# Attention values: one 64-partition load per block into a ring, the older half copied on the chip; routing's small products moved to another PSUM tile

## The chip, the cores and the metric

One core of one Trainium2 chip runs the whole program. The metric is device time in microseconds (us) of that core. "Before" stands for the kernel without the change.

## The reference

Two stages in a row, all in float32:

```python
# q, k, v: (4, 8, 768, 64)   batch, heads, tokens, head width
scores = q @ k.T / 8
keep   = (key < 4) | (0 <= query - key < 128)        # 4 sink keys and a window of 128
a      = softmax(where(keep, scores, -1e9))
x      = (a @ v), heads side by side                  # (3072, 512)
# two-level routing, top 1 at both levels, then one expert per token
g      = argmax(x @ w_group)      # 4 groups
e      = argmax(x @ w_expert[g])  # 4 experts in it
out    = p(g) * p(e) * (relu(x @ w1[g, e]) @ w2[g, e])   # 512 -> 1024 -> 512
```

## The kernel before, in words

**Attention (first third of the time).** The 3072 tokens are 24 blocks of 128 queries (`NI`; six per batch entry). One pass of the loop at line 1191, a *turn* below, works on five blocks at once in a software pipeline. In turn `i` the kernel computes the scores of block `i`, the transposes and value products of blocks `a = i-1` and `b = i-2`, the transposes of the output of block `c = i-3`, and the routing logits of block `d = i-4`. Each engine executes its instructions in program order; the order is written by hand (class `Pinned`).

In a turn TensorE (PE) runs `scores` (tile `ps`), `trans(a)` (64x64 transposes of the probabilities into the PSUM tile `tp`), `values(b, 0)` and `values(b, 1)` (into `po`), `logits(d)`, at some turns a routing product, `across(c)` and `sink_t(a)` (both into `tp`). ScalarE (ACT) copies the probabilities out of `tp` (`evac`, tile `pa`), does eight exponentials (`exps`, tile `pt`, four for each half `g` of the heads), copies the logits out (`norm_logits`, tile `lt`) between the two groups of four, and copies `tp` out once more at the end of the turn (`settle`, tile `xT`). VectorE (DVE) does masks and maxima (`maxima`, tiles `sm` and `st`), the division by the softmax sum (`norm`, tiles `rc` and `xt`), and from turn 9 on the routing of finished batches of six blocks, a fixed number of steps per turn (`routing`, `UNITS`). GpSimd (POOL) masks `pa` and `pu` (`affine_select`). SyncE (SP) issues nearly all DMAs from one queue, in program order.

`tp` has one buffer of two PSUM banks. The next turn's `trans` therefore waits until `xT` has been read out of it. Writes and reads of one PSUM bank of a tile are ordered among each other by the framework, even where they touch different columns. Before, the logits and routing's products lie in free columns of `tp` (`misc` at line 213, `logits` at 859).

**The values.** A block of 128 queries is two halves of 64. A half needs its own 64 keys, the 64 before and the 64 before those, plus the sinks. `load_v(i)` fetches a tile of 128 partitions by 2 x 520 floats (520 KB). For half 0 of the block, partitions 0 to 63 hold the block's first 64 tokens and partitions 64 to 127 the last 64 of the block before; for half 1 they hold the second and the first 64 of the block itself. So each 64-token piece is fetched twice, and the layout of the input `vN` carries it twice. `values(b, 0)` multiplies all 128 partitions. When it has read the tile, `load_s` overwrites partitions 64 to 95 with the sinks' values (130 KB), and in the next turn `values(b, 1)` reads partitions 0 to 95 of that tile. Three tiles rotate (`vts`, `vv`).

**End of attention and after it.** Lines 1252 to 1315 finish the last blocks while the first expert's layer 1 begins (`ew`). From turn 17 on, one 512 KB chunk of expert weights per turn is prefetched (`HOOK`, tile `rw`) on the same SP queue. Then the experts' products follow, layer 1 and layer 2 of one expert after another, until the end.

Of the kernel before, what the change touches and what calls it, by code (L numbers as in the profile page):

```python
# [9 lines left out]
F32 = mybir.dt.float32  # L10
# [11 lines left out]
P = 128  # L22
B, H, S, D = 4, 8, 768, 64
NT = S // P
# [6 lines left out]
NE = G * EG  # L31
# [8 lines left out]
SK = slice(D, D + NH)  # L40
# [3 lines left out]
XW = DM + GW  # L44
VW = D + 1
VM = H * VW
NEG = -1.0e30
BIG = 1 << 20
CAPT = [384, 256, 480, 288, 288, 224, 192, 192, 160, 160, 160, 160, 128, 128, 64, 32]
# [16 lines left out]
PRE = 2  # L66
# [25 lines left out]
XS = NDC * D + D  # L92
# [4 lines left out]
MAXB = 6  # L97
# [9 lines left out]
PW = G + NE  # L107
# [43 lines left out]
def moe_attention(tc, kqT, vN, vS, nsw, wg, w1, w2, out):  # L151
    nc = Pinned(tc)
    v = nc.vector
    with ExitStack() as top, ExitStack() as att:
# [37 lines left out]
        nc.gpsimd.memset(act, 0.0)  # L192
        nc.gpsimd.memset(colm[0:1], 1.0)
        nc.gpsimd.memset(kb[:, :, 0:BW], 0.0)
        vts, env, bat = {}, {}, {}

        def bank(pt):
            return pt.tile([P, 4, P], F32, name="tp")
# [11 lines left out]
        def spare():  # L210
            return tail[0].tile([P, 512], F32, name="ph")

        def misc(pt):
            if pt is None:
                return spare() if tail else env["tp"][:, 0, XS:XS + MAXB * NE + NE]
            return bank(pt).rearrange("p a b -> p (a b)")

        rawp = []
# [12 lines left out]
            for h, eng in ((slice(0, HP), nc.sync),) if i else ((slice(0, 2), nc.scalar), (slice(2, HP), nc.sync)):  # L231
                eng.dma_start(kb[:, h, n * BW:(n + 2) * BW], kqT[b, t, :, 0:KB].rearrange("d (h n) -> d h n", h=HP)[:, h])

        def room_v(i):
            vts[i] = wk.tile([P, 2, VM], F32, name="vv", bufs=3)

        def load_v(i):
            room_v(i)
            b, t = divmod(i, NT)
            nc.sync.dma_start(vts[i].rearrange("p f n -> p (f n)"), vN[b, t])  # L240

        def load_s(i):
            nc.sync.dma_start(vts[i - 1][SK].rearrange("p f n -> p (f n)"), vS[i // NT])

        for i in range(DEPTH):
            load_q(i)
# [520 lines left out]
        def maxima(i, g):  # L767
            t = i % NT
            e = env[i]
            if t:  # L770
                v.copy_predicated(psb[g][:, :, CW - D:CW], selu[:, None, :].to_broadcast([P, 4, D]), psb[g][:, :, BW - D:BW])
            e["sm", g] = sm = wk.tile([P, 4, SW], F32, name="sm", bufs=2)
            for k in range(4):
                h = head(g, k)
                v.tensor_tensor_reduce(
                    sm[:, k], psb[g][:, k, CW - SW:CW], msk[:, min(t, 2)], -0.125, 3.0e38,
                    ALU.add, ALU.min, e["st"][:, h:h + 1])

        def exps(i, g, ks=range(4)):
            e = env[i]  # L780
            for k in ks:
                h = head(g, k)
                nc.scalar.activation(e["pt"][:, h].rearrange("p (b k) -> p b k", b=2)[:, ::-1],
                                     e["sm", g][:, k].rearrange("p (b k) -> p b k", b=2), AF.Exp, bias=e["st"][:, h:h + 1],
                                     scale=-1.0)
# [43 lines left out]
                    nc.gpsimd.tensor_copy(pu[s % 2][g][SK].rearrange("p h (f q) -> p h f q", f=2),  # L829
                                          xT[SK, None, :, NDC * D:XS].to_broadcast([NH, 4, 2, D]))  # L830

        def values(i, k, gs=(0, 1)):
            rows = slice(0, P) if k == 0 else slice(0 if i % NT else D, D + NH)
            for g in gs:
                pk = env[i]["pT", g][k]
                for h in range(4):
                    for f in range(2):
                        o = slice(f * D, (f + 1) * D)
                        nc.tensor.matmul(po[o, g, h * VW:(h + 1) * VW], pk[rows, h, o],
                                         vts[i - k][rows, f, (4 * g + h) * VW:(4 * g + h + 1) * VW],  # L840
                                         start=k + h == 0, stop=k + h == 4)

        def norm(i):
# [13 lines left out]
                    nc.tensor.transpose(env["tp"][:, j, c * D:(c + 1) * D], env[i]["xt"][r, c * P:(c + 1) * P], ident[r, r])  # L857

        def logits(i):
            env[i]["lg"] = lg = spare()[:, 0:PW] if tail else env["tp"][:, 1, XS:XS + PW]  # L860
            for c in range(NDC):
                for j in range(2):
                    nc.tensor.matmul(lg[j * D:(j + 1) * D], env[i]["xT"][:, j, c * D:(c + 1) * D], wsb[:, c],
                                     start=c == 0, stop=c == NDC - 1)
# [4 lines left out]
        def norm_logits(i):  # L869
            k = max(j for j in range(len(BATCHES)) if bounds[j] <= i)  # L870
            nb, j = BATCHES[k], i - bounds[k]
            if j == 0:
                bat[k] = rk.tile([P, MAXB, PW], F32, name="lt", bufs=2)
            lt = bat[k]
            nc.scalar.copy(lt[:, j], env[i]["lg"])
            del env[i]
            have.add((id(lt), j))
            if j == nb - 1:
                pick = {SNAP: 0, SNAPB: 1, len(BATCHES) - 1: 2}.get(k)
                rb.append([[(id(lt), x) for x in range(nb)], route(bounds[k], nb, lt, pick), None])  # L880
# [303 lines left out]
                yield us  # L1184

        ew = early_work(PARTS[0][0])
        room_v(-1)
        load_s(0)
        load_v(0)
        rest = None  # L1190
        for i in range(NI):
            a, b, c, d = i - 1, i - 2, i - 3, i - 4
            state["clk"] += 3.0
            scores(i, 0)
            scores(i, 1)
            if i + DEPTH < NI:
                load_q(i + DEPTH)
            if a >= 0:
                env["tp"] = pair()
                trans(a)  # L1200
                evac(a, 0)
                evac(a, 1)
            warm(FILL[i] if i < len(FILL) else 0, po[:, 0, 300:492])
            if b >= 0:
                values(b, 0)
                load_s(b + 1)
            if i + DEPTH < NI:
                load_k(i + DEPTH)
            if i == 0:
                load_v(1)  # L1210
            if b >= 0:
                values(b, 1, (0,))
            if d >= 0:
                logits(d)
            routing(1, ("pe",))
            if b >= 0:
                values(b, 1, (1,))
                load_v(i)
            maxima(i, 0)
            exps(i, 0)  # L1220
            if d >= 0:
                norm_logits(d)
            maxima(i, 1)
            routing(PRE, (None, "rd"))
            if b >= 0:
                norm(b)
            if c >= 0:
                across(c)
            if a >= 0:
                sink_t(a)  # L1230
            exps(i, 1)
            if a >= 0:
                settle(c, a)
            if i < NI - 1:
                sink_pack(i)
            if i == 0:
                late_consts()
            if i == 3:
                tables()
            state["clk"] += 3.0  # L1240
            if rest:
                rest()
                rest = None
            put_gates(3)
            if later and not gates:
                gather(*later.pop(0))
            routing(UNITS.get(i, REND), (None, "rd"))
            rest = half.pop()() if half else wjob() if i < NI - 1 else None
            if i in HOOK:
                prefetch(min(RAW, len(raws) + 1))  # L1250
# [27 lines left out]
        sink_t(a)  # L1278
        settle(c, a)
        routing(1, ("pe",))  # L1280
        next(ew)
        if half:
            half.pop()()()
        elif state["done"] < NDC:
            wjob(True)
        values(a, 0)
        logits(c)
        env["tp"] = pair()
        across(b)
        norm_logits(c)  # L1290
        settle(b, None)
        while state["done"] < NDC:
            wjob(True)

# [287 lines left out]
def layout(q, k, v, n_sink, window, moe_w_group, moe_w_expert, moe_w1, moe_w2):  # L1582
    qT = q.reshape(B, HP, 2, NT, P, D).transpose(0, 3, 2, 5, 1, 4).reshape(B, NT, P, HP * P)
    kc = k.reshape(B, H, NT, 2, D, D)
    ks = np.broadcast_to(k[:, :, None, None, :NSK, :], (B, H, NT, 2, NSK, D))
    kx = np.concatenate([ks, ks, kc], axis=4).reshape(B, HP, 2, NT, 2, BW, D)
    kT = kx.transpose(0, 3, 2, 6, 1, 4, 5).reshape(B, NT, P, KB)
    kqT = np.concatenate([kT, qT], axis=3)
    vb = v.transpose(0, 2, 1, 3).reshape(B, NT, 2, D, DM)
    vp = np.concatenate([np.zeros_like(vb[:, :1, 1]), vb[:, :-1, 1]], axis=1)  # L1590
    vN = np.concatenate([np.concatenate([vb[:, :, 0], vp], axis=2),
                         np.concatenate([vb[:, :, 1], vb[:, :, 0]], axis=2)], axis=3)
    vN = np.concatenate([vN.reshape(B, NT, P, 2, H, D), np.ones((B, NT, P, 2, H, 1), v.dtype)], axis=5).reshape(B, NT, P, 2 * VM)
    vS = np.zeros((B, H, NSK, 2, H, VW), v.dtype)
    for h in range(H):
        vS[:, h, :, :, h, 0:D] = v[:, h, :NSK, None, :]
        vS[:, h, :, :, h, D] = 1
    nsw = np.array([n_sink, window], np.int64).view(np.int32)[None]
    wgx = np.concatenate([moe_w_group, np.ascontiguousarray(moe_w_expert.transpose(1, 0, 2)).reshape(DM, NE)], axis=1)
    wg = wgx.reshape(NDC, P, PW).transpose(1, 0, 2).reshape(P, NDC * PW)  # L1600
    return dict(kqT=kqT, vN=vN, vS=vS.reshape(B, H * NSK, 2 * VM), nsw=nsw, wg=wg,
                w1=moe_w1.reshape(NE, DM, F), w2=moe_w2.reshape(NE, F, DM))
# [17 lines left out]
```

## Time and profile before

| | |
|---|---|
| median of three runs | 492.05 us (490.28 to 492.71) |
| the profiled execution, its own time | 491.24 us |
| its span | 489.5 us |
| first scores / last value product start at | 5.1 us / 154.8 us of the span |
| granted TensorE clock, mean | 0.987 |
| busy PE / DVE / ACT / POOL | 464.7 / 366.9 / 309.0 / 167.9 us |
| DMA moved | 117.27 MB, mean 240 GB/s |

How to read it: the busy share of an engine is an average over stages with different limits, so the stretches are read one by one. In a list by time a number in brackets is idle time of the engine just before that instruction, with what ended it. The two rows' starts of the same instruction in successive turns give the length of a turn.

### The profile page before, as it was taken

The numbers are of one execution on the slowest core, as the hardware profiler recorded it, in microseconds if no ns is written. First come the engines' busy times: TensorE is split into PE (matmuls) and PEld (weight loads), VectorE is DVE, ScalarE is ACT, GpSimd is POOL, SyncE is SP. The second block draws the span as 40 slices with busy tenths as digits, with TensorE's granted clock in tenths as the row PEclk, the third lists the DMA queues.
The fourth block names the chain that finished last, engine by engine and source line by source line (L and its number), as shares of the span: only waits on it lengthen the run. The fifth ranks groups of instructions, "written<-read, shape, count | busy, mean of one in ns | idle before, by whom it ended". The sixth has DMA issues, their size and how long they took to land.

```text
span 489.5 us, 14468 instructions
## 1 busy us (share of the span) xinstructions
PE 464.7 (95%) x5427; PEld 390.9 (80%) x5427; DVE 366.9 (75%) x1181; ACT 309.0 (63%) x669; POOL 167.9 (34%) x264
## 2 busy tenths in 40 slices
PE   8999999989778999999999999999999999999993
PEld 6788888878667978988989789669776977977973
DVE  7776897898587689997823776578687997999740
ACT  4787776777484625587623765377456787788740
POOL 3675665764544112512213022212131063104102
PEclk9999999999799999999999999999999999999997
DMA  8699888998955827872963338686849983999200
GB/s 251 208 310 282 260 272 242 300 285 262 323 175 172 307 102 224 277 240 70 396 266 88 108 131 276 189 348 266 313 168 400 398 317 101 388 361 349 104 21 29
DMA packets 58833, 117.27 MB, mean 240 GB/s; under 512 B 8702, under 2 KB 20990, under 8 KB 58754
## 3 DMA queue, kind: packets, MB, share of 16 engines
q1 hardware_dynamic: 54162, 102.85, 62.3%
q0 software_dynamic: 4320, 13.26, 8.2%
q8 instruction: 45, 0.74, 0.6%
q14 instruction: 34, 0.28, 0.2%
q10 hardware_dynamic: 272, 0.15, 0.1%
HBM read 103.45 MB, written 13.03 MB: 238 GB/s over the span
## 4 chain that ended last, share of the span: by engine, by line
PE 73%; DVE 12%; ACT 6%; DMA 5%; issue 3%; SPq 1%; POOL 0%; POOLq 0%; DVEq 0%; ACTq 0%
PE ph L121 32%; PE po L121 29%; PE tp L121 7%; PE ps L121 4%; ACT pt L121 3%; DMA vv<-in_vS 2%; DVE sm L121 2%; DVE wlo L121 2%; SPq L121 1%; DMA kb<-in_kqT 1%; ACT pa L121 1%; DVE xt L121 1%; DVE un L121 1%; ACT whi L121 1%; DMA out<-ot,hidx 1%
## 5 line engine op out<-in xcount | busy, mean ns | idle before, releaser
L121 DVE TENSOR_TENSOR wlo<-rw,whi 128x1024 fp32r<-128x1024 f32 x112 | 134.3, 1219 | 26.5 <-ACT whi L121 25.5
L121 PE MATMUL po<-whi,un 128*128 128x512 f32 (+5 forms) x384 | 127.9, 396 | 0.0
L121 PE MATMUL ph<-un,whi 128*128 128x256 f32 (+9 forms) x576 | 127.6, 312 | 0.0
L121 ACT CAST whi<-rw 128x1024 fp32r<-128x1024 f32 (+1 forms) x115 | 115.3, 1026 | 8.4 <-PE po L121 4.3
L121 POOL DMA_INDIRECT out<-ot,sidx x32 | 42.1, 1316 | 228.4 <-ACT ot L121 88.8
L121 PE MATMUL ph<-un,wlo 128*128 128x256 f32 (+10 forms) x416 | 99.3, 264 | 0.7 <-DVE wlo L121 0.7
L121 PEld LDWEIGHTS ph<-un,whi 128*128 128x128 f32 x576 | 93.6, 189 | 1.2
L121 PEld LDWEIGHTS po<-whi,un 128*128 128x128 f32 (+4 forms) x384 | 70.4, 185 | 25.2 <-issue 6.7
L121 PEld LDWEIGHTS ph<-un,wlo 128*128 128x128 f32 x416 | 76.7, 189 | 1.6 <-DVE wlo L121 0.9
L121 PE MATMUL po<-wlo,un 128*128 128x512 f32 (+6 forms) x200 | 77.5, 389 | 0.0
L121 ACT ACTIVATE pt<-sm,st 128x136 f32<-128x136 f32 x192 | 61.9, 401 | 8.3 <-DVE st L121 8.2
L121 DVE CUSTOM_DVE_ANT_0 sm<-ps,msk 128x136 f32<-128x136 f32 x192 | 45.9, 295 | 5.2 <-PE ps L121 0.2
L121 POOL DMA_INDIRECT xg<-xd,gidx x30 | 33.5, 1115 | 26.2 <-DMA rw<-in_w 12.9
L121 PEld LDWEIGHTS po<-wlo,un 128*128 128x128 f32 (+5 forms) x200 | 36.0, 180 | 7.7
L121 ACT COPY pa<-tp 128x512 f32<-128x512 f32 x48 | 25.8, 589 | 25.2 <-PE tp L121 25.2
L121 POOL COPY pu<-xT 32x512 f32<-32x512 f32 x46 | 28.0, 636 | 39.2 <-ACT xT L121 33.5
L121 PE MATMUL ps<-kb,qb 64*64 64x208 f32 (+1 forms) x768 | 39.3, 345 | 0.5 <-DMA kb<-in_kqT 0.5
L121 DVE TENSOR_TENSOR hc<-ph,hc 128x160 f32<-128x160 f32 (+6 forms) x64 | 21.1, 335 | 22.2 <-ACT hc L121 22.0
L121 PE MATMUL po<-vv,pu 96*64 96x65 f32 (+1 forms) x768 | 32.2, 227 | 3.9 <-DMA vv<-in_vS 3.7
L121 ACT ACTIVATE ot<-po,cg 128x512 f32<-128x512 f32 (+6 forms) x25 | 17.0, 679 | 26.5 <-PE po L121 26.5
L121 ACT ACTIVATE un<-ph 128x256 fp32r<-128x256 f32 (+1 forms) x40 | 15.3, 383 | 26.9 <-PE ph L121 26.2
L121 PEld LDWEIGHTS ps<-kb,qb 64*64 64x64 f32 x768 | 27.5, 139 | 5.8 <-DVE st L121 0.7
(203 smaller groups left out, 686.6 us busy)
## 6 DMA issues: line engine op xcount, KB each, us to landing
rw<-in_w SPq DMA_DIRECT2D x128, 512.0 KB, 6.2
vv<-in_vN SPq DMA_DIRECT2D x24, 520.0 KB, 5.1
kb<-in_kqT SPq DMA_DIRECT2D x23, 288.0 KB, 4.6
qb<-in_kqT SPq DMA_DIRECT2D x24, 256.0 KB, 4.8
xd<-xt SPq DMA_DIRECT2D x24, 256.0 KB, 4.9
vv<-in_vS SPq DMA_DIRECT2D x24, 130.0 KB, 3.8
out<-ot,sidx POOLq DMA_INDIRECT x32, 4.0
xg<-xd,gidx POOLq DMA_INDIRECT x30, 4.0
```

Source lines behind the costliest of these rows:

```text
L121: r = f(*a, **k)
```

## The change

`load_v(i)` fetches each 64-token piece once: 64 partitions by 2 x 520 floats, 260 KB, into partitions 0 to 63 of two slots of a ring of six (`vv`, the same size as the three tiles before). A new step `older(i)` copies, on the chip, the piece before each half into partitions 64 to 127 of its slot: 64 partitions by 1040 floats in one instruction, or in two of 520 where the ring wraps. VectorE does it for blocks 0 to 8, ScalarE from block 9 on. In a turn it stands behind both `maxima` in program order, on ScalarE between the two groups of exponentials, and it needs the load of block `i-1` to have landed.

The logits and routing's small products move from free columns of `tp` to free columns of `po`. The copy of the logits, `lt`, moves from ScalarE to VectorE, behind `norm`. `values(b, 1)` runs without `logits` in its middle, `load_v(i)` is issued behind it and thus ahead of `logits`, and routing's reads of its products are no longer among the two steps taken ahead of `norm`. At the end, `values(a, 0)` comes later.

```diff
+NV = 6
+OLDER = 9
...
-                return spare() if tail else env["tp"][:, 0, XS:XS + MAXB * NE + NE]
+                return spare() if tail else po[:, 0, 4 * VW:4 * VW + MAXB * NE + NE]
...
-        def room_v(i):
-            vts[i] = wk.tile([P, 2, VM], F32, name="vv", bufs=3)
+        vv = wk.tile([P, NV, VM], F32, name="vv", bufs=1)

         def load_v(i):
-            room_v(i)
             b, t = divmod(i, NT)
-            nc.sync.dma_start(vts[i].rearrange("p f n -> p (f n)"), vN[b, t])
+            s = 2 * i % NV
+            nc.sync.dma_start(vv[0:D, s:s + 2].rearrange("p f n -> p (f n)"), vN[b, t])
...
+        def older(i):
+            copy = v.tensor_copy if i < OLDER else nc.scalar.copy
+            s = 2 * i % NV
+            if i % NT == 0:
+                copy(vv[D:P, s:s + 2], vv[0:D, s:s + 2][:, ::-1])
+            elif s:
+                copy(vv[D:P, s:s + 2], vv[0:D, s - 1:s + 1])
+            else:
+                copy(vv[D:P, 0], vv[0:D, NV - 1])
+                copy(vv[D:P, 1], vv[0:D, 0])
...
-            env[i]["lg"] = lg = spare()[:, 0:PW] if tail else env["tp"][:, 1, XS:XS + PW]
+            env[i]["lg"] = lg = spare()[:, 0:PW] if tail else po[:, 1, 4 * VW:4 * VW + PW]
...
-            nc.scalar.copy(lt[:, j], env[i]["lg"])
+            (nc.scalar.copy if tail else v.tensor_copy)(lt[:, j], env[i]["lg"])
...
             if b >= 0:
-                values(b, 1, (0,))
+                values(b, 1)
+                load_v(i)
             if d >= 0:
                 logits(d)
             routing(1, ("pe",))
-            if b >= 0:
-                values(b, 1, (1,))
-                load_v(i)
             maxima(i, 0)
             exps(i, 0)
+            maxima(i, 1)
+            if a >= 0:
+                older(a)
+            routing(PRE, (None,))
+            if b >= 0:
+                norm(b)
             if d >= 0:
                 norm_logits(d)
-            maxima(i, 1)
-            routing(PRE, (None, "rd"))
-            if b >= 0:
-                norm(b)
...
         routing(1, ("pe",))
+        older(a)
...
-        values(a, 0)
         logits(c)
         env["tp"] = pair()
         across(b)
         norm_logits(c)
         settle(b, None)
+        values(a, 0)
```

## Rows read from the trace of the kernel before

**Rows 1.** Busy time by stretch; window, length, engines, granted clock, DMA share, GB/s.

```profile
54.70:113.00 58.30, 54.26 (x1407) 47.10 (x1403) 51.58 (x264) 43.38 (x124) 36.23 (x63) 1.00 0.88 265
113.00:134.00 21.00, 17.80 (x372) 14.76 (x374) 15.07 (x78) 12.59 (x34) 12.54 (x20) 0.84 1.02 319
...
157.00:198.00 41.00, 39.82 (x274) 34.59 (x271) 32.76 (x115) 18.41 (x32) 7.72 (x6) 1.00 0.63 213
```

**Rows 2.** ScalarE in order of time, one turn; start, length, instruction.

```profile
30.39 1.08 ACT L121 COPY pa<-tp 128x512 f32<-128x512 f32 x2 [1.12 <-PE tp L121]
31.34 1.31 ACT L121 ACTIVATE pt<-sm,st 128x136 f32<-128x136 f32 x4
32.55 0.16 ACT L121 COPY lt<-tp 128x20 f32<-128x20 f32 x1
32.61 1.31 ACT L121 ACTIVATE pt<-sm,st 128x136 f32<-128x136 f32 x4
33.82 0.68 ACT L121 COPY xT<-tp 128x640 f32<-128x640 f32 x1
```

**Rows 3.** TensorE in order of time, the same turn.

```profile
29.63 0.71 PE L121 MATMUL tp<-ident,pt 64*128 64x64 f32 x16
...
31.79 0.63 PE L121 MATMUL tp<-wsb,xT 128*64 128x20 f32 x16
...
34.55 0.65 PE L121 MATMUL tp<-ident,pt 64*128 64x64 f32 x14
```

**Rows 4.** Turns from `trans` to `trans`, columns as in rows 1.

```profile
56.31:62.78 6.47, 5.66 (x149) 4.85 (x146) 6.08 (x31) 4.53 (x13) 4.41 (x9) 1.00 0.88 282
62.78:67.94 5.16, 4.80 (x144) 4.27 (x140) 4.84 (x29) 4.32 (x12) 3.28 (x6) 1.00 0.85 244
...
85.35:90.60 5.25, 5.25 (x144) 4.60 (x140) 4.27 (x24) 4.11 (x12) 3.87 (x8) 1.00 0.98 304
...
96.96:101.88 4.92, 4.74 (x143) 4.27 (x139) 4.57 (x27) 4.11 (x12) 3.38 (x7) 1.00 0.78 238
101.88:108.51 6.63, 5.42 (x138) 4.60 (x138) 6.42 (x32) 4.50 (x13) 4.14 (x8) 1.00 1.01 312
...
115.32:120.86 5.54, 5.54 (x142) 4.72 (x138) 4.57 (x23) 4.74 (x13) 3.87 (x8) 1.00 0.97 276
```

**Rows 5.** ScalarE in order of time, the turn from 101.88.

```profile
105.08 1.31 ACT L121 ACTIVATE pt<-sm,st 128x136 f32<-128x136 f32 x4 [1.38 <-DVE st L121]
```

**Rows 6.** TensorE in order of time, the longest turn, from 120.86.

```profile
125.56 1.10 PE L121 MATMUL po<-vv,pu 96*64 96x65 f32 x16 [2.90 <-DMA vv<-in_vS]
...
129.04 3.05 PE L121 MATMUL ps<-kb,qb 64*64 64x208 f32 x32
```

**Rows 7.** Groups by form: engine, operation, tiles, shapes, count, busy us, mean ns, idle before.

```profile
L121 ACT CAST whi<-rw 128x1024 fp32r<-128x1024 f32 x109 | 111.6, 1048 | 8.4 <-PE po L121 4.3 <-DMA rw<-in_w 3.9
...
L121 ACT CAST whi<-rw 128x512 fp32r<-128x512 f32 x6 | 3.7, 620 | 0.0
...
L121 DVE COPY cnt<-tp 128x16 f32<-128x16 f32 x2 | 0.3, 164 | 0.0
...
L121 DVE COPY msk<-msk 128x136 f32<-128x136 f32 x1 | 0.2, 230 | 0.0
```

**Rows 8.** VectorE in order of time, the turn of rows 2.

```profile
31.75 0.29 DVE L121 CUSTOM_DVE_ANT_0 sm<-ps,msk 128x136 f32<-128x136 f32 x1
...
32.96 0.17 DVE L121 TENSOR_SCALAR rc<-po 128x8 f32<-128x8 f32 x1 [0.90 <-PE po L121]
```

**Rows 9.** VectorE in order of time: one operation beside GpSimd's masks, and without them.

```profile
103.43 0.55 DVE L121 TENSOR_TENSOR rm<-req,rs 128x24 f32<-128x24 f32 x1
...
176.70 0.18 DVE L121 TENSOR_TENSOR rm<-req,rs 128x24 f32<-128x24 f32 x1
```

**Rows 10.** Instructions on tile `tp`: who its writers waited for, us and times.

```profile
  ACT lt L121: 8.4, 9
```

**Rows 11.** DMA issues: count, KB each, median us from issue to landing.

```profile
vv<-in_vN SPq DMA_DIRECT2D x24, 520.0 KB, 5.1
...
vv<-in_vS SPq DMA_DIRECT2D x24, 130.0 KB, 3.8
```

More of the change, by code (lines that the diff above doesn't have):

```diff
@@ L194, in moe_attention @@
         nc.gpsimd.memset(kb[:, :, 0:BW], 0.0)
-        vts, env, bat = {}, {}, {}
+        env, bat = {}, {}
         def bank(pt):
@@ L232, in load_k @@
                 eng.dma_start(kb[:, h, n * BW:(n + 2) * BW], kqT[b, t, :, 0:KB].rearrange("d (h n) -> d h n", h=HP)[:, h])
-        def room_v(i):
-            vts[i] = wk.tile([P, 2, VM], F32, name="vv", bufs=3)
+        vv = wk.tile([P, NV, VM], F32, name="vv", bufs=1)
         def load_v(i):
-            room_v(i)
             b, t = divmod(i, NT)
-            nc.sync.dma_start(vts[i].rearrange("p f n -> p (f n)"), vN[b, t])
+            s = 2 * i % NV
+            nc.sync.dma_start(vv[0:D, s:s + 2].rearrange("p f n -> p (f n)"), vN[b, t])
         def load_s(i):
-            nc.sync.dma_start(vts[i - 1][SK].rearrange("p f n -> p (f n)"), vS[i // NT])
+            s = 2 * (i - 1) % NV
+            nc.sync.dma_start(vv[SK, s:s + 2].rearrange("p f n -> p (f n)"), vS[i // NT])
+        def older(i):
[8 more added lines that the diff above has]
+                copy(vv[D:P, 1], vv[0:D, 0])
         for i in range(DEPTH):
@@ L830, in settle, with values @@
                                           xT[SK, None, :, NDC * D:XS].to_broadcast([NH, 4, 2, D]))
-        def values(i, k, gs=(0, 1)):
+        def values(i, k):
             rows = slice(0, P) if k == 0 else slice(0 if i % NT else D, D + NH)
-            for g in gs:
+            for g in range(2):
                 pk = env[i]["pT", g][k]
@@ L839, in values @@
                         nc.tensor.matmul(po[o, g, h * VW:(h + 1) * VW], pk[rows, h, o],
-                                         vts[i - k][rows, f, (4 * g + h) * VW:(4 * g + h + 1) * VW],
+                                         vv[rows, 2 * (i - k) % NV + f, (4 * g + h) * VW:(4 * g + h + 1) * VW],
                                          start=k + h == 0, stop=k + h == 4)
@@ L1186, in moe_attention @@
         ew = early_work(PARTS[0][0])
-        room_v(-1)
         load_s(0)
@@ L1589, in layout @@
     vb = v.transpose(0, 2, 1, 3).reshape(B, NT, 2, D, DM)
[L1590 to L1593, printed above, removed]
+    vN = vb.transpose(0, 1, 3, 2, 4)
+    vN = np.concatenate([vN.reshape(B, NT, D, 2, H, D), np.ones((B, NT, D, 2, H, 1), v.dtype)], axis=5).reshape(B, NT, D, 2 * VM)
     vS = np.zeros((B, H, NSK, 2, H, VW), v.dtype)
```

## The prediction

> **What bounds the kernel now.** I read the busy time by stretch first, then single turns in order of time, then prices. By stretch [rows 1]: behind attention (157 to 198 us) TensorE is busy 39.82 of 41.00 us, so the end of attention hands its delay on one to one. [...] In a plain turn TensorE and ScalarE run neck and neck. ScalarE's chain is closed: it starts 0.76 us after `trans` (30.39 against 29.63), runs `pa`, four exponentials, `lt`, four exponentials and `xT` without a gap until 34.50, and the next `trans` starts 0.05 us later, at 34.55 [rows 2, 3]. That is a turn of 4.92 us, and the reader is to see that nothing on ScalarE in it is slack but the 1.12 us ahead of `pa`. TensorE's own work makes most other turns some 5.2 to 5.5 us. From turn 10 on VectorE has routing to do: turns with much of it take 6.5 to 6.6 us, in which VectorE is busy 6.1 to 6.4 us and ScalarE waits 1.38 us for `st` [rows 4, 5]. [...]
>
> **The copy on ScalarE, turns 10 to 23.** `older` copies 1040 floats per partition. ScalarE's nearest rows are copies of 512 (620 ns) and 1024 (1048 ns) from on-chip memory [rows 7]: 0.836 ns per float, so 1.06 us. Instructions behind each other overlap by 0.1 us (`pa` runs to 31.47, the exponentials start at 31.34; the next start 32.55 lies ahead of 32.65) [rows 2], so the copy adds 0.95 us to the chain; `lt` leaves and gives 0.06 us back (32.55 to 32.61). ScalarE's closed chain becomes 4.92 - 0.06 + 0.95 = 5.81 us. Eleven turns go from `trans` at 56.31 to `trans` at 120.86, 5.87 us on average [rows 4]. Five are shorter than 5.81: 5.16, 5.54 (twice, one shown), 5.25 and 4.92 [rows 4]. Lifted to 5.81 they cost 0.65 + 0.27 + 0.56 + 0.89 + 0.27 = 2.6 us. In the VectorE-bound turns the copy is behind a late `st`, between the two groups of exponentials, and the second group waits for its own maxima; there part of it is free, and part comes on top. On the other hand VectorE can work ahead while ScalarE is late: in a 5.81 us turn it gets 0.3 to 0.9 us that it did not have in the short ones, and the 6.63 us turns shrink. Least: the long turns average out with the short, eleven times 5.81 = 63.9 against 64.55 us, -0.6. Most: 0.95 in each of eleven turns, +10.5. I take +2.0, near the lifted short turns, since the turns that VectorE bounds leave little to average.
>
> **The copy on VectorE, turns 1 to 9.** Its copies take 164 ns for 16 floats and 230 ns for 136 [rows 7], that is 0.55 ns per float and 0.73 us for 1040. VectorE has a hole for it in a plain turn: `sm` ends at 32.04 and `rc` waits 0.90 us for the value products until 32.96 [rows 8]. The copy fits, if the load has landed. If it runs beside GpSimd's masks, which fill that part of the turn, it may wait: the same small operation took 0.55 us there and 0.18 us without them [rows 9], so 0.37 us more, 1.10 us, and 0.20 over in each of seven turns that are not a batch's first. `lt` adds 0.16 us behind `norm` (the row of 16 floats, [rows 7]), where VectorE has the rest of the hole. Bounds 0 and +1.4 us (with 1.04 ns per float, twice the slope, +5); I take +0.5.
>
> [...]
>
> **The load.** `older` is the first reader of `load_v(a)`; before it was `values(a, 0)` in the turn after. The load is issued earlier, right behind `values(b, 1)` and ahead of the 0.63 us of `logits` [rows 3]. The SP queue order is `load_q`, `load_s`, `load_k`, `load_v`, output, so nothing else moves in it. Issue is some 3 us behind `trans`; 5.1 us of landing [rows 11] puts it 8 us behind, and ScalarE reaches `older` 2.9 us into the next turn, 8.7 us behind in a turn of 5.81. VectorE reaches it 2.4 us in, 7.6 us behind. The wait is thus 0 to 0.5 us; behind it stand four exponentials and `xT` on ScalarE, `norm` on VectorE. With half the bytes I take 0.
>
> **DMA.** The saving is 260 KB per turn. At the 319 GB/s of the full stretch [rows 1] that is 0.82 us each; three value loads fall into the 21 us, so up to -2.4 us where DMA sets the time, and nothing elsewhere, because before 113 us the loads land in time. But the load now writes 64 partitions. The sinks' load writes 32, and its 130 KB land in 3.8 us against 5.1 us for 520 KB [rows 11]: a quarter of the bytes, three quarters of the time. Bounds -2.4 and 0; I take -1.2.
>
> **The move out of `tp`.** `across` no longer waits for the reading of `lt` or of routing's products (8.4 us in 9 waits, shared between weight loads and products, so about half as much time) [rows 10]. It would start `sink_t` and the next scores sooner by up to 0.7 us in some five turns. But `xT` now ends later than before on ScalarE, and `trans` waits for `xT`, so the gain is eaten: 0, at best -1.5 us. In `po` the next `values(b, 0)` has to wait for `lt` and for routing's reads on VectorE; these end about 1 us ahead of it. At the end of attention `older(a)` puts 1 us in front of ScalarE's casts, and `values(a, 0)` moves behind; the sinks' load is still the last to land there. 0, at most +1.
>
> **Sum.** +2.0 + 0.5 + 0 - 1.2 + 0 = +1.3 us. On the profiled execution (491.24 us) that is 492.5, on the median (492.05) 493.4. I predict 492.9 us, and call the change within 0.5% (2.5 us), about what a measurement of this kernel tells from no change.
>
> **Rivals.**
>
> *ScalarE's chain sets every turn (slower).* Place: the stretch from turn 10. It decides if VectorE's routing can't work ahead, since both `maxima` and the copy then come in series: in the turn from 101.88 the exponentials start late [rows 5], then copy, exponentials and `xT` follow, +0.9 us. The price is the 2.6 us of the short turns, 0.6 to 0.9 us in four heavy turns (3.0) and a late landing here and there (1): +6.5, about 498 us. For it: ScalarE's chain has no gap [rows 2]. Against: VectorE is busy 51.58 of 58.30 us from 54.7 to 113 us, 5.2 us per average turn [rows 1]. Chance 0.23.
>
> *The DMA stall goes (faster).* The 2.90 us wait goes if the sinks' load lands 3 us sooner, and with it the slow products behind it: 1.4 us of scores alone [rows 6], some 3 us in all with the products ahead. -6 + 1.3 gives 487.3 us. For it: the full queues. Against: ahead of that load in the queue are weights and queries, not values. Chance 0.29.
>
> *A load into 64 partitions holds the DMA engines as long as one into 128.* Then the 1.2 us of relief go: 494.1 us. For it: rows 11. Against: a small load also has a part of its landing that no bytes cause. Chance 0.10.
>
> [...]
>
> **How the numbers follow.** The forecast has 0.38; its own range is 490 to 496 (0.04 faster, 0.26 same, 0.08 slower). The slow rival gives 0.21 slower and 0.02 same, the fast one 0.27 faster and 0.02 same, the third 0.05 and 0.05. Sums: 0.31 faster, 0.35 same, 0.34 slower. The range reaches to both outer rivals and a little beyond: 486 to 499.
>
> **What would show it.** Right: in the changed trace `vv<-vv` takes near 1.05 us on ScalarE and 0.7 to 1.1 on VectorE; plain turns from 10 on are near 5.8 us with `trans` right behind `xT`; VectorE shows no wait for `in_vN`; DMA share in the full stretch falls; no `tp` wait for `lt`. Wrong: turns 10 to 20 below 5.6 us on average (the chain is not closed), or idle time on ScalarE or VectorE ahead of `vv` for `in_vN` (the landing), or the attention's first ten turns longer by over 2 us (the copy does not fit the hole), or a stall near 120 us that is gone or has doubled.

## The result and the profile after

In 20 runs each the changed kernel takes 494.48 us (median; 490.98 to 498.26) and the kernel before 491.74 us: a ratio of 1.0055 with a 95% interval of 1.0028 to 1.0082, that is 2.7 us more. Every ratio below is the time over that of the kernel before, with such an interval behind it. The profiled execution has a span of 492.4 us against 489.5.

The stretches of [rows 1], now of the changed kernel, same columns:

```profile
54.70:113.00 58.30, 49.83 (x1313) 42.97 (x1311) 48.54 (x256) 48.20 (x115) 34.37 (x61) 1.00 0.75 210
113.00:134.00 21.00, 16.85 (x420) 14.49 (x420) 16.77 (x82) 18.20 (x43) 10.38 (x18) 1.00 0.96 266
157.00:198.00 41.00, 41.00 (x325) 35.75 (x320) 37.21 (x119) 19.14 (x33) 5.67 (x5) 1.00 0.66 224
```

In the first stretch every engine but ScalarE does less in the same 58.30 us: TensorE 49.83 us instead of 54.26, ScalarE 48.20 instead of 43.38. The DMA share falls from 0.88 to 0.75. Turns from `trans` to `trans`, as in [rows 4]:

```profile
56.68:64.89 8.21, 5.81 (x150) 4.66 (x146) 7.61 (x35) 5.46 (x14) 3.75 (x7) 1.00 0.74 220
64.89:70.95 6.06, 4.70 (x138) 4.26 (x138) 5.60 (x31) 5.36 (x13) 3.91 (x7) 1.00 0.67 193
...
77.01:83.07 6.06, 5.98 (x144) 5.23 (x144) 3.84 (x24) 5.20 (x12) 1.37 (x3) 1.00 0.67 178
```

Of eleven turns (`trans` at 56.68 to 126.24) nine lie between 6.05 and 6.15 us, one is 6.67 and the first 8.21. Before, the same eleven ran from 4.92 to 6.80 us. One number that keeps coming back, whatever the other engines have to do, is the mark of a closed chain. ScalarE in order of time, the turn from 77.01, beside [rows 2]:

```profile
77.77 1.07 ACT L123 COPY pa<-tp 128x512 f32<-128x512 f32 x2 [0.80 <-PE tp L123]
78.73 1.31 ACT L123 ACTIVATE pt<-sm,st 128x136 f32<-128x136 f32 x4
80.06 1.06 ACT L123 COPY vv<-vv 64x1040 f32<-64x1040 f32 x1
81.14 1.30 ACT L123 ACTIVATE pt<-sm,st 128x136 f32<-128x136 f32 x4
82.35 0.67 ACT L123 COPY xT<-tp 128x640 f32<-128x640 f32 x1
83.83 1.07 ACT L123 COPY pa<-tp 128x512 f32<-128x512 f32 x2 [0.81 <-PE tp L123]
```

The copy costs 1.06 us as worked out. But the exponentials ahead of it end at 80.04 and it starts at 80.06; it ends at 81.12 and the next start at 81.14. Between exponentials and `xT` the usual overlap of 0.1 us is there (82.35 against 82.44). So the copy adds 80.06 to 81.14 and the lost overlap, 1.20 us instead of 0.95, and the loop is 6.06 us. Of the chain of waits ScalarE now holds 10% (before 6%). TensorE's side says the same: what instructions on tile `tp` waited for (us and times):

```profile
  ACT xT L123: 34.0, 33
```

The same row of the kernel before:

```profile
  ACT xT L121: 9.6, 18
```

The wait for `xT` has more than tripled; `lt` of [rows 10] is gone from the list. The copies on tile `vv` (count, lowest/median/highest ns, first and last start), and what they waited for:

```profile
L123 ACT COPY vv<-vv x18: 618/1057/1060, 61.8 to 155.1; 64x1040 f32<-64x1040 f32 x12, 64x520 f32<-64x520 f32 x6
L123 DVE COPY vv<-vv x10: 419/696/1026, 12.5 to 54.3; 64x1040 f32<-64x1040 f32 x8, 64x520 f32<-64x520 f32 x2
...
  DMA vv<-in_vN: 5.2, 6
```

The loads, as in [rows 11], and TensorE in the stall of [rows 6]:

```profile
vv<-in_vN SPq DMA_DIRECT2D x24, 260.0 KB, 5.1
...
vv<-in_vS SPq DMA_DIRECT2D x24, 130.0 KB, 4.1
```

```profile
128.87 1.15 PE L123 MATMUL po<-vv,pu 96*64 96x65 f32 x32 [0.83 <-DMA vv<-in_vS]
...
137.24 1.25 PE L123 MATMUL po<-vv,pu 96*64 96x65 f32 x32 [1.37 <-POOL pu L123]
...
139.30 3.05 PE L123 MATMUL ps<-kb,qb 64*64 64x208 f32 x32
```

Where the 2.9 us of the span come from, by the starts of `trans` and the end of the last value product: up to the tenth `trans` +0.4 (56.31 to 56.68), the eleven turns +5.0 (64.55 to 69.56), the rest of attention -2.1 (34.1 to 32.1 us). That is 3.3 us at the end of attention (155.0 to 158.3), of which the stage behind it gives 0.4 back. These are differences of one trace each. The place alone and the four kernels with a spare copy (below) are the same program up to the tenth turn, and their tenth `trans` starts between 55.12 and 56.62 us: a difference of half a us, such as the +0.4, says nothing by itself.

### The profile page after: what moved, and what is told of

It is laid out like the page before. It is cut to its first block, busy times and chain, and to the rows that moved or that the text cites. A ratio compares the mean times of both kernels' runs of the same rounds, so it can differ in the third digit from the quotient of the medians.

```text
span 492.4 us, 14530 instructions
## 1 busy us (share of the span) xinstructions
PE 463.6 (94%) x5427; PEld 389.7 (79%) x5427; DVE 375.4 (76%) x1211; ACT 323.4 (66%) x667; POOL 167.9 (34%) x264
## 4 chain that ended last, share of the span: by engine, by line
PE 70%; DVE 11%; ACT 10%; DMA 4%; issue 3%; SPq 1%; POOL 0%; POOLq 0%; DVEq 0%; ACTq 0%
PE ph L123 31%; PE po L123 30%; PE tp L123 6%; ACT pt L123 5%; PE ps L123 2%; DMA vv<-in_vN 2%; DVE wlo L123 2%; DVE sm L123 2%; ACT xT L123 1%; ACT vv L123 1%; ACT pa L123 1%; DVE un L123 1%; DVE xt L123 1%; DMA kb<-in_kqT 1%; ACT whi L123 1%
## 5 line engine op out<-in xcount | busy, mean ns | idle before, releaser
L123 POOL DMA_INDIRECT out<-ot,sidx x32 | 43.5, 1361 | 228.1 <-ACT ot L123 90.1
L123 POOL COPY pu<-xT 32x512 f32<-32x512 f32 x46 | 26.9, 611 | 49.2 <-ACT xT L123 44.0
L123 POOL DMA_INDIRECT xg<-xd,gidx x30 | 32.1, 1070 | 24.8 <-DMA rw<-in_w 12.2
L123 ACT COPY hc<-ph 128x160 f32<-128x160 f32 (+6 forms) x64 | 19.4, 304 | 18.1 <-PE ph L123 17.1
L123 PEld LDWEIGHTS tp<-ident,pt 64*128 64x128 f32 x384 | 13.9, 139 | 21.9 <-ACT xT L123 20.7
```

The source lines that it names most:

```text
L123: r = f(*a, **k)
```

## The experiments

**One half alone.** First the move into `po` with its new order, on the old 128-partition loads, without any copy; then the ring with its copies, with logits and routing's products left in `tp`.

```diff
 # kernel before, place and order alone
-  ... else env["tp"][:, 1, XS:XS + PW]
+  ... else po[:, 1, 4 * VW:4 * VW + PW]      # routing's products likewise, lt on VectorE
 # changed kernel, ring alone
-  ... else po[:, 1, 4 * VW:4 * VW + PW]
+  ... else env["tp"][:, 1, XS:XS + PW]       # routing's products likewise, lt on ScalarE
```

> Half of the change: logits and routing's products in po, lt on VectorE, the new order; values loaded as before, 128 partitions, no copy. Theory (ScalarE's chain): the eleven turns take 58 to 60 us, ratio 0.998 to 1.002; the turn from block 10 still long (near 8 us) if routing's later start makes that one. Rival (VectorE): eleven turns near 63 us and ratio 1.004 to 1.006. If the stall near 120 us stays as before, the new load is what shortened it.

> The other half: the ring, the 64-partition load and the copies; logits and routing's products stay in tp, lt on ScalarE, the old order. Theory (ScalarE's chain): copy and lt both in it, 6.1 us per turn, eleven turns 64 us or more, ratio 1.005 to 1.010. Rival (VectorE): eleven turns near 59 us, ratio 1.000 or below.

Measured: place and order alone 488.57 us, ratio 0.9956 (0.9929 to 0.9982); ring alone 498.19 us, ratio 1.0163 (1.0128 to 1.0198). The first is better and the second worse than either theory had it. The change is a gain of 0.4% and a loss. With the place the ring costs 1.0055 - 0.9956, about 1.0% or 4.9 us; without it 1.6%. ScalarE with the ring alone, by time:

```profile
83.79 1.31 ACT L123 ACTIVATE pt<-sm,st 128x136 f32<-128x136 f32 x4
85.11 0.18 ACT L123 COPY lt<-tp 128x20 f32<-128x20 f32 x1
85.31 1.06 ACT L123 COPY vv<-vv 64x1040 f32<-64x1040 f32 x1
86.39 1.30 ACT L123 ACTIVATE pt<-sm,st 128x136 f32<-128x136 f32 x4
```

`lt` stands in the same closed chain, and the eleven turns are 6.12 to 6.90 us. The theories' "eleven turns" near 63.5 us are the ten from the tenth `trans` to the twentieth: 63.49 us in the changed kernel, 58.83 with the place alone, 64.16 with the ring alone, as the theory of ScalarE's chain had them. Place and order alone beats both kernels.

The expectation for the place alone named a test of the smaller loads: if the stall near 120 us stays as before, the new load is what shortened it. It did not stay. With full loads the wait for the sinks' values is 1.82 us instead of 2.90, and the three turns from the twentieth `trans` to the 23rd take 22.0 us instead of 23.4:

```profile
123.87 1.15 PE L121 MATMUL po<-vv,pu 96*64 96x65 f32 x32 [1.82 <-DMA vv<-in_vS]
```

**The copy elsewhere on ScalarE.** Only the turn's ScalarE copy moves, behind `xT`.

```diff
-            if a >= 0:
+            if 0 <= a < OLDER:
                 older(a)
...
                 settle(c, a)
+            if a >= OLDER:
+                older(a)
```

> Only ScalarE's copy moves: from between the two groups of exponentials to behind xT, where ScalarE waits some 0.75 us for the next transposes anyway. Theory (ScalarE's closed chain of 6.06 us sets the turns): the chain drops to about 5.25 us, the eleven turns after turn 10 from 63.5 to some 59 to 60 us, the time by 3 to 4 us, to 0.997 to 1.000 of before. Rival (VectorE: the moved lt and routing's later start): the turns stay near 63 us, ratio 1.005. Rival (landing of the value loads): the later copy waits less, but the loads also come earlier in a shorter turn; at most 1 us better, ratio 1.003 to 1.005.

Measured: 491.26 us, ratio 1.0013 (0.9986 to 1.0040), 0.4% under the changed kernel, whose interval overlaps this one at its edge; the theory had 0.997 to 1.000. The copy still runs and costs the same time; it no longer stands ahead of `trans`. ScalarE by time:

```profile
85.41 0.68 ACT L123 COPY xT<-tp 128x640 f32<-128x640 f32 x1
86.11 1.06 ACT L123 COPY vv<-vv 64x1040 f32<-64x1040 f32 x1
87.45 1.07 ACT L123 COPY pa<-tp 128x512 f32<-128x512 f32 x2 [0.28 <-PE tp L123]
88.41 2.50 ACT L123 ACTIVATE pt<-sm,st 128x136 f32<-128x136 f32 x8
```

It lies in the time in which ScalarE waits for the next `trans` anyway, and the turns are 5.10 to 6.20 us again, with one of 7.10 and one of 8.29 (TensorE idles for 1.67 us in it, for no reason that the trace shows). The ten turns take 61.6 us, against 63.5 in the changed kernel and 59 to 60 expected. In this profile the stall ahead of 136 us grew to 4.96 us, for `pu` from GpSimd (a turn of 12.93 us), so the attention stage as a whole shows less of the gain than the turns do:

```profile
136.04 2.00 PE L123 MATMUL po<-vv,pu 96*64 96x65 f32 x32 [4.96 <-POOL pu L123]
```

**No copy at all.** The changed kernel without `older`; the upper partitions hold zeros, so only the attention stage is read.

> The changed kernel without the copies (the upper partitions hold zeros, so attention's output, routing and the number of tokens per expert differ; only the attention stage is to be read). Theory: turns of 5.2 to 5.6 us where VectorE has little routing, eleven turns 57 to 60 us. Rival (VectorE): near 63 us. For the load: if 64 partitions hold the queues as long as 128, the DMA share in plain turns stays near 0.87; if bytes count, it is near 0.77.

Measured: ten turns (from the tenth `trans` to the twentieth) take 58.53 us; the kernel before takes 59.01, the changed one 63.49. The stage from the fourth `trans` to the tenth takes 30.83 us, against 32.17 both before and after; the place alone and the four spare-copy kernels below, with full loads and no copy up to there, take 30.95 to 32.03, so that is no clear gain. This kernel is the place alone with the smaller loads, and the place alone takes 58.83 us for the ten turns: the smaller loads make nothing slower here, and nothing clearly faster. From 60 to 112 us the DMA share is 0.77 at 223 GB/s, against 0.86 at 269 with the place alone.

**The copy without the ring.** The kernel with the place alone, and a spare copy on ScalarE where `older` stands, from turn 10 on, into an idle end of another tile; from partitions 0 to 63 into 0 to 63, then into 64 to 127.

```diff
+            if a >= 9:
+                nc.scalar.copy(un[0:D, (NDC + NFC) * W - 2 * VM:], vts[a][0:D]...)   # then un[D:P, ...]
             routing(PRE, (None,))
```

> The half with po alone (values loaded as before, right output) and in it one spare ScalarE copy per turn from turn 10 on, where the changed kernel has its copy: 64 partitions by 1040 floats from partitions 0 to 63 to partitions 0 to 63 of an idle region. Theory (a copy that starts on another partition than its neighbours can't overlap them): this one overlaps by 0.1 us at both ends, the chain is 4.86 + 0.95 = 5.81 us, eleven turns from block 10 take 66 to 67 us, ratio near 1.000. Rival (every copy of this size costs 1.2 us in the chain): plain turns 6.06 us, eleven turns 68 to 69.5 us, ratio 1.003 to 1.006. If the turns stay at 5.1 to 5.5 us, the chain is not what sets them.

> The same spare copy, but into partitions 64 to 127. Theory: no overlap at either end, plain turns 6.05 us as in the changed kernel, eleven turns 68 to 69.5 us, ratio 1.002 to 1.006, some 2.5 us slower than the spare copy into partitions 0 to 63. Rival (destination does not matter): both alike. If both are alike and well below the changed kernel, the load and not the copy makes its turns long.

Measured: low 493.36 us, ratio 1.0029 (1.0003 to 1.0054); high 493.90 us, ratio 1.0045 (1.0021 to 1.0068). Against the place alone that is +0.7% and +0.9% of the ring's 1.0%, with no load changed. By time alone low and high can't be told apart (the expectation had 2.5 us between them), and the low copy's ratio is nearer to the rival's 1.003 than to the theory's 1.000; the loops tell them apart. Low:

```profile
82.28 1.05 ACT L121 CAST un<-vv 64x1040 fp32r<-64x1040 f32 x1
83.23 1.31 ACT L121 ACTIVATE pt<-sm,st 128x136 f32<-128x136 f32 x4
84.44 0.67 ACT L121 COPY xT<-tp 128x640 f32<-128x640 f32 x1
85.92 1.07 ACT L121 COPY pa<-tp 128x512 f32<-128x512 f32 x2 [0.81 <-PE tp L121]
86.88 1.31 ACT L121 ACTIVATE pt<-sm,st 128x136 f32<-128x136 f32 x4
88.14 1.06 ACT L121 CAST un<-vv 64x1040 fp32r<-64x1040 f32 x1
```

High:

```profile
84.17 1.06 ACT L121 CAST un<-vv 64x1040 fp32r<-64x1040 f32 x1
85.25 1.30 ACT L121 ACTIVATE pt<-sm,st 128x136 f32<-128x136 f32 x4
86.46 0.67 ACT L121 COPY xT<-tp 128x640 f32<-128x640 f32 x1
87.94 1.07 ACT L121 COPY pa<-tp 128x512 f32<-128x512 f32 x2 [0.81 <-PE tp L121]
88.90 1.31 ACT L121 ACTIVATE pt<-sm,st 128x136 f32<-128x136 f32 x4
90.23 1.06 ACT L121 CAST un<-vv 64x1040 fp32r<-64x1040 f32 x1
```

In the low copy the exponentials start 0.10 us ahead of its end (83.23 against 83.33), and most turns are 5.80 to 5.92 us: the 5.81 of the prediction. In the high copy they start 0.02 us behind it (85.25 against 85.23), and turns are 6.06.

**What takes the overlap.** The same spare copy, from partitions 64 to 127 into 64 to 127, and into 0 to 63.

> Spare ScalarE copy of 64x1040 from turn 10 on, as in the runs with a spare copy, but from partitions 64 to 127 into partitions 64 to 127. The copy's output is not used; everything else computes as before. Theory A (what removes the 0.1 us overlap at both ends of the copy is that its output lies on other partitions than its input): here input and output partitions are the same, so the exponentials start some 0.1 us before the copy's end, and undisturbed turns are near 5.81 us. Theory B (any copy that does not begin at partition 0 loses the overlap, its neighbours all begin there): 6.06 us, no overlap. The profile decides, one look is enough.

> The same spare copy from partitions 64 to 127 into partitions 0 to 63. Theory A (shift between input and output): no overlap, turns near 6.06 us. Theory B as 'output begins above 0': overlap, 5.81 us; theory B as 'input begins above 0': none, 6.06 us.

Measured: one run each, 494.86 and 494.29 us beside 493.11 of the kernel before; the times of single runs decide nothing, the loops do. High into high, then high into low, by time:

```profile
83.06 1.31 ACT L121 ACTIVATE pt<-sm,st 128x136 f32<-128x136 f32 x4
84.39 1.06 ACT L121 CAST un<-vv 64x1040 fp32r<-64x1040 f32 x1
85.48 1.30 ACT L121 ACTIVATE pt<-sm,st 128x136 f32<-128x136 f32 x4
```

```profile
84.95 1.06 ACT L121 CAST un<-vv 64x1040 fp32r<-64x1040 f32 x1 [0.33 <-DMA vv<-in_vN]
86.03 1.31 ACT L121 ACTIVATE pt<-sm,st 128x136 f32<-128x136 f32 x4
```

Both lose it (84.37 and 84.39; 86.01 and 86.03), and plain turns are 6.06 in both. At the front end a wait hides it in the second kernel; one turn earlier its copy starts 0.03 us behind the exponentials (78.57 against 78.54). A shift between input and output is not what does it: theory A falls. An input or an output that starts at partition 64, between neighbours that start at 0, is enough. The kernel before shows it too, at copies into partitions 64 to 95, and I had not looked for it:

```profile
135.69 1.29 ACT L121 ACTIVATE pt<-sm,st 128x136 f32<-128x136 f32 x4
137.01 1.06 ACT L121 COPY pu<-tp 32x512 f32<-32x512 f32 x2
138.09 0.58 ACT L121 COPY xT<-tp 128x512 f32<-128x512 f32 x1
138.57 0.62 ACT L121 CAST whi<-rw 128x512 fp32r<-128x512 f32 x1
```

The two `pu` copies begin 0.03 us behind the exponentials and end 0.02 us ahead of `xT`; `xT` and `whi`, both from partition 0, overlap by 0.09 us.

**All copies on VectorE.** `OLDER = 24` instead of 9.

> The changed kernel with all 24 copies on VectorE. ScalarE's chain then has no copy, 4.86 us. Theory (ScalarE's chain): turns without routing fall to 5.2 to 5.6 us, but where VectorE has routing its 0.7 us come on top: the eleven turns 62 to 66 us, ratio 1.000 to 1.006. Rival (VectorE has room, since 0.75 us fitted its hole in the first turns): 59 to 60 us, ratio 0.996 to 0.999.

Measured: 500.08 us, ratio 1.0165 (1.0136 to 1.0193), slower than any theory had it. Its stretch from 54.7 us, columns as in [rows 1]:

```profile
54.70:113.00 58.30, 50.68 (x1283) 43.22 (x1280) 53.70 (x241) 37.17 (x98) 34.55 (x62) 0.97 0.70 197
```

ScalarE falls to 37.17 us and VectorE is busy 53.70 of 58.30: turns are 5.10 to 7.74 us, 6.68 on average over the eleven (57.04 to 130.56). VectorE's hole of the first nine turns is gone once routing fills it.

**The place without its moves.** The place alone, but with `lt` on ScalarE between the groups of exponentials, as before, and routing's reads back in the steps taken ahead of `norm`. `values(b, 1)` stays in one piece, with `load_v` behind it.

> The half with po alone, but lt still on ScalarE between the two groups of exponentials, and routing's reads again among the two steps ahead of norm. Theory (the gain of that half is that the transposes into tp no longer wait for readers of lt and of routing's products): the place alone gives it, ratio 0.995 to 0.998. Rival (the gain is the move of lt and of the reads off the way of the exponentials): ratio 0.999 to 1.002.

Measured: 491.35 us, ratio 0.9982 (0.9955 to 1.0010). It lies between the kernel before and the place with its moves, and the intervals cover both. How the 0.4% divides between the place and the moves stays open.

## Why the prediction came out as it did

The forecast was 492.9 us; the new runs give 494.48. The sum of +1.3 us stands against +2.9 in the profiled executions and +2.7 in the medians. The sign was right, and the time lies between the forecast and the slow rival. By the number alone the third rival (494.1) came nearest, but not by its mechanism, as shown below. That the sum missed by only 1.6 us is in part luck: the term of ScalarE's copy was 3.0 us too low, and 0.9 at the end of attention, 0.4 behind it and 0.1 in the first turns went the other way. Step by step:

- **The copy on ScalarE, taken at +2.0: +5.0 in the eleven turns.** This is the term that was mis-sized. The copy's price of 1.06 us was exact, and that the chain is closed was right. The step that failed is "instructions behind each other overlap by 0.1 us, so the copy adds 0.95 us": it adds 1.20, and the loop is 6.06 instead of 5.81. At 6.06 six short turns of before (5.15, 5.78, 5.55, 5.24, 4.92, 5.55) cost 4.2 us instead of 2.6 (the forecast counted five and left out 5.78, which at 5.81 is worth 0.03). VectorE did work ahead, as argued, but three longer turns gave back only 1.0 us (6.37 to 6.15, 6.80 to 6.07, 6.09 to 6.05), and the first grew by 1.7. The spare copy shows the term had the overlap held: ten turns (from the tenth `trans` to the twentieth) go from 58.83 to 61.24 us, +2.4. With the overlap lost they take 61.88, 63.37 and 64.79 us in the three other spare copies, +3.1 to +6.0; the loop of 6.06 us is the same in all three, and the rest is single long turns, which scatter from trace to trace. So the lost overlap is shown in the loop, while its share of the +5.0 is an estimate, some 1.6 us (4.2 - 2.6).
- **The first turn, 6.47 to 8.21 us.** It is the slow rival's mechanism in one place: exponentials start late, then the copies follow in series, on ScalarE by time:

```profile
60.45 1.30 ACT L123 ACTIVATE pt<-sm,st 128x136 f32<-128x136 f32 x4 [1.94 <-DVE st L123]
61.78 1.15 ACT L123 COPY vv<-vv 64x520 f32<-64x520 f32 x2
62.95 1.30 ACT L123 ACTIVATE pt<-sm,st 128x136 f32<-128x136 f32 x4
```

  VectorE was late with routing's first steps. The high spare copy shows 0.60 us of that wait and a turn of 6.78, so about 1.4 us of the 8.21 are neither the copy's price nor its overlap. Some of VectorE's steps there took 0.74 and 0.66 us against 0.28 and 0.26 in the spare run; whether GpSimd's masks, which ran beside them, made them slow was not tried. Nor is this turn's length the copy's alone: it takes 6.19 us with the place alone, 7.10 where the copy stands behind `xT` or on VectorE, and 7.40 with one of the spare copies.
- **The copy on VectorE, taken at +0.5: +0.4 in the first ten turns, which lies within the scatter of these turns.** It takes 0.70 us in the median (0.73 worked out) and at most 1.03, and lies in the hole of [rows 8]. The 1.04 ns per float of the upper bound is, in the trace of before, the slope of VectorE's `un<-tp,un` (286 ns for 128 floats, 685 for 512).
- **The landing, taken at 0:** six copies, three on each engine, waited 5.2 us in all for `in_vN`. In the changed kernel half the bytes land no sooner, in 5.1 us. On VectorE that cost nothing that stands out of the scatter of the first ten turns; ScalarE's share of it is in the turns already counted.
- **DMA, taken at -1.2: -2.1 from the end of the eleven turns to the end of attention.** The sinks' wait falls from 2.90 to 0.83 us, but the next turn waits 1.37 us for GpSimd's `pu`, and there the 32 score products take 3.05 us, as before. The mean granted clock, as a share of full speed, moved with the stall: from 113 to 134 us it is 1.00 instead of 0.84, from 134 to 157 us 0.85 instead of 1.00. The stall moved rather than went; the fast rival's 6 us were not to be had. The -2.1 lies within the forecast's bounds, but the reason given for it, the smaller loads, is not borne out: from the twentieth `trans` to the 23rd the place alone, with full loads, takes 22.0 us, the changed kernel 22.1, the kernel before 23.4, the ring alone, with small loads, 24.7. With full loads the spare copies, low and high, show no wait of 0.7 us or more for the sinks at all, and take 30.4 and 30.1 us for the rest of attention, less than the changed kernel's 32.1. The relief is there without the smaller loads, with the place and with longer turns; which of these brings it stays open.
- **The load into 64 partitions (third rival).** Between 54.7 and 113 us bytes fall to 210 / 265 = 0.79 and the DMA share to 0.75 / 0.88 = 0.85. Part of that is longer turns. At nearly equal turns, without copies against the place alone, bytes fall to 223 / 269 = 0.83 and the share to 0.77 / 0.86 = 0.90. Some of the engines' time does go with the bytes, so the rival falls as stated; for the landing time it had the better guess. The part of a landing that no bytes cause, held against it, is there in the trace of before: 8 KB (`xd<-cw`) take 3.4 us to land, 130 KB 3.8.
- **The move out of `tp`, taken at 0: -2.2 us alone (0.44%).** "The gain is eaten" holds only where the copy is there to eat it. I had priced the parts each against the kernel with all others in it, and so missed that one part alone was worth having.

The views named ahead answered as hoped: 1.06 us and 0.7 to 1.0 us for the copies, `trans` right behind `xT`, no wait for `lt`, a lower DMA share. "Plain turns near 5.8 us" and "no wait for `in_vN`" failed.

## What to carry to other kernels

Where one engine's chain is closed around the loop, each instruction that enters it lifts every shorter turn to the new loop (here six turns of 4.92 to 5.78 us to between 6.06 and 6.08); put it behind the instruction that the next turn waits for (here behind `xT`, 0.4% cheaper) instead of ahead of it. Before an overlap with the neighbours is counted, look in the trace of before for an instruction of the same engine that starts at the same partition. And time the parts of a change alone: here one part is 0.4% faster than the kernel before, and the other takes back more than twice that.

## What the runs showed of the hardware

- In the low spare copy's loops (5.80 to 5.92 us) ScalarE's instructions all start at partition 0 and overlap by 0.1 us. At a copy whose input or output starts at partition 64 neither end overlaps: it starts 0.02 to 0.03 us behind the exponentials, and the next start 0.02 to 0.03 us behind it (loops of 6.06 us: the changed kernel and three of the spare copies); two such copies behind each other do overlap (1.15 us for two of 0.62).
- 260 KB into 64 partitions land in 5.1 us in the median in the changed kernel, no sooner than 520 KB into 128 before; in three of the experiments they take 4.4 to 5.0 us, and the 520 KB of the place alone 5.7. The DMA share falls (0.86 to 0.77 at nearly equal turns).
- Ahead of 142 us TensorE waits for GpSimd's `pu` in the changed kernel (1.37 us) and in seven of the experiments (1.21 us with the low spare copy to 4.96 with the copy behind `xT`), and not in the kernel before. That `pu` copy starts 0.12 us behind the landing of an indirect gather issued earlier in GpSimd's queue, in the kernel before (131.01 against 130.88 us) and in the changed one (136.52 against 136.40); in the seven experiments the profile ends its idle time, 2.88 to 5.16 us, with the same gather. The four masks between the two ran without that wait (in the changed kernel from 129.85 to 132.57 us); why the copy waits was not tried. In the kernel with the place alone GpSimd, and then TensorE:

```profile
132.23 1.16 POOL L121 COPY pu<-xT 32x512 f32<-32x512 f32 x2 [4.84 <-DMA xg<-xd,gidx]
```

```profile
132.88 1.25 PE L121 MATMUL po<-vv,pu 96*64 96x65 f32 x32 [2.15 <-POOL pu L121]
```
